# Chunk-select attention and a gated MLP on one core: an earlier load order, more k, q and v buffers, a new order of all engines, and a last output tile in two halves

## The chip, the core and the metric

The kernel runs on one core of one Trainium2 chip. Its engines work side by side: TensorE (PE: matmuls, and PEld: its weight loads), VectorE (DVE), ScalarE (ACT), GpSimd (POOL, which here issues all loads) and SyncE (SP, which here issues transposing transfers, copies between buffers and stores). The metric is the device time of one execution in microseconds, the median of several runs.

## The reference, cut to what is computed

Inputs: q, k, v of shape (4, 8, 768, 64), and weights w_in (512, 1024), w_spatial (768, 768), b_spatial (768), w_out (512, 512), all float32. Output: (4, 768, 512) float32.

```python
k_min, k_max = k_chunks.min(3), k_chunks.max(3)            # 24 chunks of 32 keys
ub = sum_d max(q * k_min, q * k_max)                        # a bound for each query and chunk
top_chunks = argsort(where(causal_chunk, ub, -1e9))[..., -6:]
scores = where(in_top_chunks & causal, q @ k.T / 8, -1e9)
x = softmax(scores) @ v                                     # heads side by side: (4, 768, 512)
h = relu(x @ w_in);  u, v = h[..., :512], h[..., 512:]
v_n = (v - mean(v)) / sqrt(var(v) + 1e-6)
v_s = einsum('ts,bsd->btd', w_spatial, v_n) + b_spatial[:, None]
out = (u * v_s) @ w_out
```

## The kernel before, in words

**Tiling.** Tokens go in tiles of 128, so a sequence has six. Heads are worked in pairs: 16 pairs i, four to a batch (0 to 3 are batch 0), two to a load group g = i // 2. After four pairs have filled a batch's x, the MLP of that batch runs while the pairs of the next batch go on. The MLP of the last batch has nothing beside it.

**The order is written out by hand.** The string ORDER is a list of short names, and each name stands for one small function that issues one or a few instructions on one engine. The kernel body ends with a loop that calls them in this order. Each engine then works through its own names strictly in that order, and waits where an operand or a buffer is not there yet. Engines are tied only by data and by buffers. The function build lists each name with its engine, its dependences and the buffers that it takes; PLAN holds its parameters (buffer counts, and a list of names, `flip`, whose engine is exchanged between ACT and DVE).

**The names**, for pair i, head hi (0 or 1) and batch b, with lines of the kernel before:

- Loads on POOL: `lk`, `lq`, `lv` with g and, for k and q, a half (L589, L595, L600; eight smaller ones for g = 0 at L604), `win` (eight, L608), `wsp` (six, L624), `wout` (four, L626), `lb` (L627). The k loads go into 4 buffers, q into a ring of 4, v into a ring of 4. A q buffer also holds the selection bits beside q, whose place `ring` (DVE, L532) clears once; `small` sets a column of ones in each v buffer (L546) and some constants.
- Bounds: `kT` transposes k on PE (L665; `kTb` again into another bank for pairs 0 and 1, L674), `kmax` and `kmin` reduce it to chunks (DVE, L686), `kb` spreads them (L708), `qT` transposes q (L722; `qTb` L679), `rq` takes its positive and negative parts (L731, L733, or ACT), `ub` multiplies (L742), `top` finds the eight largest of each row (DVE, L752), `sel` compares and writes the selection next to q (L778).
- Operands of the scores: `kop` copies k.T (L717) or, from pair 8 on, `kc` copies it (L703) and `kop` moves it on by a transfer from SP (L715); `kh` puts the mask rows into the k operands once (L574). `aT` transposes q with its selection on PE (L797; `aTA`, `aTB` in parts for pair 0, L785), `ac` copies it (L800; L790, L792 for pair 0); from pair 8 on one transposing transfer `aTd` on SP does both (L803).
- Attention: `sc` scores in six strips (L810, and L813 for the triangle in batch 0), `ex` exp (ACT, L819), `tri` clears the upper triangle from batch 1 on (POOL, L825), `av` in three parts (L836), `rc` and `nm` normalise (DVE, L841, L846), `x` brings x.T to the MLP (transfer on SP, L855; for pairs 0 to 3 and 15 `xp` on PE, L861, and a DVE copy, L864).
- MLP, tile ti: `v` and `u` (x times w_in), `s` (times w_spatial), `o` (times w_out), all matmuls at L930; `va` and `ua` relu on ACT (L947, L962); `bs`, `vs`, `rs`, `vn` normalise; `gt` the gate on DVE (L973, three buffers), `gd` its transposing transfer on SP (L988; for the last two tiles `gp` on PE and a copy, L980, L986), `oc` copies the output out of PSUM (L993), `os` stores it (L997). `wsT` and `wsc` transpose w_spatial once (L634, L636).
- `dm`: matmuls of zeros into a spare bank, 65 of them, between the first instructions of PE (L873).

**What sets the order around the change.** POOL issues loads and triangles in one order, so a load that stands behind a triangle waits for that pair's exps. SP issues `aTd`, `kop`, `x`, `gd` and `os` in one order. PE, DVE and ACT likewise. PSUM has 3 banks for scores, 1 for small transposes and bounds, 1 for av, 3 for the MLP and, in batch 0, for transposes.

Of the kernel before, what the change touches and what calls it, by code (L numbers as in the profile page):

```python
# [166 lines left out]
def mmc(n): return max(n/2.4+2.5,25)/1000  # L167
DEF=dict(BEATS=12,pa=8,dve_a=(),qx=('ACT',),xp=4,mlp_first=13,mlp_mul=1.0,sc=3,tr=1,acc=1,ml=3,kbuf=3,qbuf=3,vbuf=3,ebuf=3,late=240,chunk=2,
  lk=40,lq=36,lv=18,kdma=99,kcp=2,kcdma=1,kc_act=(),shift=4,prep=0.0,tm=.8,lm=0.2,lm2=1.2,gp=(),head=1,lag=0.0,kp=27,ca=99,tree=0,svk=1.4,svw=1.15,flip=(),wide=0,pt=(),xd=(),dum=0,warm0=0.,qa_dve=(),ma_act=(),mkbuf=2)
PEL=0.2  # L170
def build(prm=None):
# [19 lines left out]
    for x in range(2):  # L191
        for hi in range(2):
            op(f'lk0{hi}{x}','POOL',.815,acq=[('k',0)],prio=B0-1+2*x+.1*hi,dma=(.85,1.8))
            op(f'lq0{hi}{x}','POOL',.815,acq=[('qs',0)],prio=B0-.5+2*x+.1*hi,dma=(.85,1.8))
# [16 lines left out]
    for i in range(NPAIR):  # L211
# [34 lines left out]
        for hi in range(2):  # L246
            if (kd or kc) and p['kcdma']:
                op(f'kop{i}{hi}','SP',.5,deps=[kt],acq=[('kh',i)],uses=[kr],prio=pr((3 if hi==0 else 8)),dma=(.45,1.8))
            else:
                ke='ACT' if i<2 else 'DVE'  # L250
                kq=('acc',f'kb{i}') if kdup else kr
                op(f'kop{i}{hi}',ke,(.80 if ke=='ACT' else .46) if not tree else .30,.1,deps=[f'kTb{i}' if kdup else kt],acq=[('kh',i)],uses=[kq],prio=pr((3 if hi==0 else 8)))
# [69 lines left out]
    for b in range(B):  # L322
# [5 lines left out]
        o_=[group('o',b,ti,4,lambda c0,m,ti=ti: [f'gd{b}{ti}']+[f'wout{j}' for j in range(KO)],[('gT',f'{b}{ti}')]) for ti in range(NQT)]  # L328
# [32 lines left out]
    for b in range(B):  # L361
        for ti in range(NQT):
            q=s.ops[last('o',b,ti,4)].prio
            op(f'oc{b}{ti}','ACT',.465,.12,deps=[last('o',b,ti,4)],acq=[('o',f'{b}{ti}')],uses=[('ml',f'o{b}{ti}')],prio=q+.5)
            op(f'os{b}{ti}','SP',.5,deps=[f'oc{b}{ti}'],uses=[('o',f'{b}{ti}')],prio=q+.6,dma=(.7,1.6))
# [6 lines left out]
    for o in s.order:  # L372
        if o.name[:2]=='kh': o.alts=('DVE',.32)
        elif o.name[:3]=='kop' and o.eng=='ACT': o.alts=('DVE',.46)
        elif o.name=='rq01' and o.eng=='ACT': o.alts=('DVE',.40)
    for n in p['flip']:
        o=s.ops[n]; e,oc=o.alts; o.alts=(o.eng,o.occ); o.dur+=oc-o.occ; o.eng,o.occ=e,oc
    for k in range(p['dum']): op(f'dm{k}','PE',mmc(128),PEL,deps=['dz'],acq=[('sc','dm')] if k==0 else [],uses=[('sc','dm')],prio=-22+k*.15)
# [3 lines left out]
PLAN = {'late': 40, 'mlp_first': 8, 'qbuf': 4, 'kbuf': 4, 'vbuf': 4, 'dum': 65, 'warm0': 5.3, 'kcp': 8, 'flip': ['ac21', 'ac60', 'ac71', 'gd34', 'kc11', 'kc13', 'kc14', 'kc9', 'kh01', 'kh31', 'oc00', 'oc01', 'oc11', 'oc12', 'oc13', 'oc20', 'oc22', 'rq01'], 'gp': ((3, 4), (3, 5)), 'lm': 0.2, 'lm2': 1.2, 'tm': 0.8}  # L382

ORDER = """
dz id0 dm50 ring0 dm19 dm26 lk000 dm35 dm14 dm55 dm53 ring1 dm13 dm36 dm49 lk010 dm6 dm1 small dm46 dm60 ring2 lq010
ring3 lq000 id1 lk011 expand lk001 kT0 kh31 kh30 dm40 dm7 lq001 dm56 dm31 dm3 kmin0 dm62 kTb0 kh21 lq011 qT0 kmax0
kh20 dm27 dm10 dm15 qTb0 lk10 dm42 dm38 dm41 dm48 kh01 dm30 dm8 dm57 kop01 rq00 rq01 mlat kop00 kT1 lk11 kb0 dm54 dm11
dm43 dm44 dm24 kmax1 dm32 dm52 dm45 kh00 dm0 ub0 kTb1 lv0 top00 dm20 dm47 dm2 dm23 kh11 dm34 dm29 dm58 dm59 dm28 kmin1
dm4 dm5 dm25 dm63 dm61 dm39 dm64 dm22 qT1 kh10 mtri dm18 dm33 dm21 top01 dm51 dm37 dm17 dm16 selA0 kop10 lq10 sel0
aTA00 rq11 aTB0 dm12 rq10 dm9 kop11 lq11 acA00 aTA01 kb1 sc000 acB0 ub1 lk20 ex000 sc001 top10 sc002 ex001 sc004 acA01  # L390
kT2 lq20 ex002 top11 sc003 ex004 sel1 sc011 kop20 lk30 av000 ex003 sc005 kop21 ex011 sc013 kmax2 lq21 aT10 ex005 ex013
aT11 av001 kmin2 ac10 sc010 lk21 av002 ex010 sc100 rc00 kb2 qT2 nm00 ac11 win01 kT3 rq21 sc015 wsp3 sc012 ex100 rq20
qT3 wsp5 ex015 kmax3 sc102 ex012 sc014 lv1 ex102 sc112 kmin3 ub2 ex014 av010 sc101 ex112 top20 sc111 lk41 ex101 av011
rq31 sc103 av012 ex111 top21 sc104 lk31 rc01 ex103 sel2 sc113 kb3 ex104 rq30 sc105 aT20 nm01 ex113 sc115 lv2 ub3 kop31
ex105 av100 ac20 sc114 top30 av101 sc110 ex115 kop30 ex114 av102 lq30 sc203 top31 ex110 aT21 rc10 sel3 sc200 ex203
nm10 win30 sc202 qT4 ex200 ac21 kT4 ex202 win21 sc205 rq40 sc201 aT30 kmax4 ex205 ex201 sc215 sc212 av110 ex215 win00
kmin4 ex212 sc211 av111 sc210 ac30 av112 rq41 aT31 ex211 kb4 sc204 kop40 ub4 ex210 sc214 kop41 ex204 rc11 sc213 top40
kT5 ex214 lq31 nm11 sc300 ac31 xp0 top41 av200 kmin5 ex213 av201 sc301 ex300 av202 sel4 xp1 ex301 rc20 sc310 kmax5
sc311 wsp2 ex310 qT5 sc302 win31 nm20 ex311 sc303 rq51 ex302 av210 rq50 ex303 av211 kop51 sc305 aT40 ex305 kop50 av212
sc304 ac40 x0 sc313 kT6 win20 rc21 ex304 kb5 aT41 nm21 sc315 ex313 sc312 kmax6 ex315 sc404 ac41 win11 sc314 x1 xp2  # L400
ex312 win10 av300 kmin6 ub5 ex404 av301 sc401 lk61 ex314 top50 sc402 av302 ex401 sc403 top51 wsp0 rc30 ex403 sc400
sel5 nm30 ex402 aT50 kop61 av310 ac50 lk40 x2 av311 sc412 ex400 kop60 sc405 qT6 av312 kb6 ex412 wsp4 sc415 rq60 kT7
ex405 rc31 sc413 ex415 rq61 sc411 tri40 sc501 nm31 ex413 aT51 kop70 ex411 av400 lq41 xp3 kmax7 ac51 av401 sc410 av402
wsp1 ex501 x3 sc414 ub6 ex410 kmin7 sc502 v00.0 ex414 sc503 kop71 ex502 v00.2 tri41 rc40 sc504 top60 sc500 v02.0 ex504
nm40 wout1 v04.0 ex503 top61 lq40 av410 va00 sel6 v02.2 qT7 lk50 va02 v04.2 rq71 av411 ex500 sc514 rq70 av412 va04
sc511 bs00 aT60 ex514 v01.0 rc41 ac60 ex511 sc510 v03.0 vs00 kb7 ex510 bs02 sc600 ub7 ex600 v01.2 nm41 sc505 sc515
top70 v03.2 x4 ex505 va01 av500 top71 tri50 sc513 ex515 sc603 sel7 va03 wsT0 bs01 wout0 ex513 av501 aT61 wsc0 ex603
lv3 av502 sc602 wsT1 rc50 ac61 vs02 bs04 sc512 v05.0 ex602 wsc1 aT70 ex512 kT8 nm50 sc613 ac70 v05.2 kmin8 tri51 sc604
sc601 va05 av510 vs04 lk71 kc8 u01.0 ex604 kmax8 av511 ex601 qT8 lv4 u01.2 ex613 rq81 u00.0 ua01 vs01 rq80 sc611 sc605
sc610 bs03 ex611 lq50 u00.2 aT71 bs05 ua00 av512 wsT2 kb8 ex605 sc614 ac71 wsT3 tri60 ex614 wsc2 sc704 ub8 ex610 wsc3  # L410
wsT4 lk51 u02.0 vs05 ex704 rc51 vs03 top80 sc703 rs0 u02.2 lq51 nm51 ex703 sc612 wsT5 wsc4 ex612 av600 lb top81 sc701
ua02 sc700 vn04 u03.0 ex701 wsc5 sc702 av601 ex700 vn00 u04.0 ex702 vn01 u03.2 sel8 av602 sc615 u04.2 ua03 vn03 aTd8
kT9 ex615 vn02 ua04 sc705 s00.0 tri61 rc60 ex705 nm60 sc710 kc9 sc713 vn05 s00.2 tri70 kop80 ex710 av610 kmin9 x5
sc715 s00.4 ex713 wout2 u05.0 kmax9 lq60 av611 kop81 sc711 av612 qT9 kop90 ex711 rc61 s01.0 nm61 ex715 u05.2 rq91
av700 rq90 ua05 s01.2 kb9 sc714 gt00 av701 ub9 ex714 sc712 gd00 av702 top90 s02.0 rc70 s01.4 top91 sc803 sel9 kop91
s02.2 gt01 ex803 sc800 aTd9 kT10 ex712 nm70 s02.4 ex800 kmin10 sc805 qT10 tri71 ex805 sc801 gd01 sc810 kmax10 s03.0
ex801 wout3 av710 ex810 sc802 gt02 x6 sc804 av711 ex802 sc812 kc10 av712 ex804 s03.2 rc71 ex812 s04.0 kop100 nm71
tri80 sc814 kb10 gd02 sc815 rq101 kT11 ex815 s03.4 lq61 rq100 ex814 sc811 kmax11 av800 x7 ex811 s04.2 gt03 av801 sc813
av802 ub10 kop101 ex813 rc80 s05.0 kc11 sc900 tri81 sc905 sc901 nm80 s05.2 kop110 ex901 top100 lk60 s04.4 ex900 gd03
av810 gt04 s05.4 ex905 av811 sc911 kmin11 sc904 o00.0 ex911 av812 gt05 ex904 sc903 sc910 o00.2 top101 ex910 sc912  # L420
sel10 o02.0 ex903 oc00 aTd10 qT11 ex912 o01.0 rq111 sc902 rc81 o02.2 kb11 ex902 rq110 kop111 o01.2 nm81 oc02 ub11 gd04
tri90 v10.0 oc01 sc913 v11.0 lq70 x8 v10.2 v13.0 lv5 va10 sc914 v11.2 bs10 v13.2 va11 av900 v14.0 ex913 bs11 av901
va13 v12.0 top110 ex914 sc1002 av902 top111 v14.2 ex1002 bs13 o03.0 va14 v12.2 rc90 sel11 sc915 vs10 sc1000 nm90 va12
kT12 aTd11 o03.2 vs11 ex1000 kc12 v15.0 ex915 bs14 oc03 sc1003 tri91 sc1001 gd05 av910 kmin12 ex1001 v15.2 lq71 u10.0
# [35 lines left out]
def kernel(  # L460
# [407 lines left out]
    for n in range(prm["dum"]):  # L868
        @act(f"dm{n}")
        def warm(n=n):  # L870
            if "warm" not in tiles:
                tiles["warm"] = ps_sc.tile([P, 512], F32, tag="sc", name="warm")
# [135 lines left out]
    for b in range(B):  # L1008
        mlp(b)
# [33 lines left out]
```

## Time and profile before

| | |
|---|---|
| median of 6 runs | 204.19 us (202.82 to 204.53) |
| the profiled execution's own time | 205.19 us |
| its span, first to last instruction | 203.5 us |
| granted TensorE clock, mean | 0.995 |
| PE / DVE / ACT / POOL busy | 189.5 / 157.6 / 147.4 / 79.7 us |
| HBM read, written | 24.38 MB, 6.29 MB |

The profile is of one execution. Its page gives, for each engine, the busy time, then the span in 40 slices of about 5.1 us with the busy share of each in tenths, then the chain of work that ended last, followed back from the end, then the costliest groups of instructions. The trace behind it can be asked for a stretch of time, for the waits of an engine, and for the time from the issue of a transfer to its landing. A line such as `87.67 7.06 DMA gT<-g` of the chain means that from 87.67 us on the chain spent 7.06 us on that transfer. In a wait line the numbers are the total time, how often, and the longest.

### The profile page before, as it was taken

The page shows a single profiled execution, that of the slowest core. Times are in us where ns is not written, and L with a number is a line of the kernel's source. Part 1 is how long each engine was busy: PE and PEld are TensorE (multiplying, and loading weights), DVE is VectorE, ACT ScalarE, POOL GpSimd, SP SyncE. Part 2 cuts the span into 40 slices and gives each one's busy share as a digit, 9 for nine tenths or more (in the row PEclk, how much of TensorE's full clock was granted, in tenths as well). Part 3 has the DMA queues.
Part 4 walks back from the last instruction along what each step waited for, and adds up shares of the span by engine and source line. Part 5 has one row for each costly group of instructions (what it writes and reads, how often), then busy time and mean ns, then how long its engine had stood idle before and what let it go on. Part 6 is the DMA issues. An engine that isn't in the chain of part 4 may idle for free.

```text
span 203.5 us, 5218 instructions
## 1 busy us (share of the span) xinstructions
PE 189.5 (93%) x2012; PEld 119.2 (59%) x2012; DVE 157.6 (77%) x476; ACT 147.4 (72%) x292; POOL 79.7 (39%) x96
## 2 busy tenths in 40 slices
PE   3897999999999999997999999999899999999991
PEld 2885678767576756663555655565455555444440
DVE  6898899999899999986688968795687466467530
ACT  2877999899799994875498958688799470564142
POOL 7999774257637853360614321304303030000000
PEclk9999999999999999999999999999999999999998
DMA  6999999999999999999999997969964172250355
GB/s 41 104 128 152 156 165 140 165 176 151 123 110 104 142 119 185 153 171 136 144 147 154 155 251 197 100 170 175 174 156 152 26 193 59 73 208 0 72 187 209
DMA packets 114617, 28.60 MB, mean 141 GB/s; under 512 B 108704, under 2 KB 111008, under 8 KB 114592
## 3 DMA queue, kind: packets, MB, share of 16 engines
q0 software_dynamic: 76544, 12.20, 91.6%
q1 hardware_dynamic: 38048, 16.06, 37.8%
q8 instruction: 16, 0.26, 0.6%
q14 instruction: 9, 0.07, 0.1%
HBM read 24.38 MB, written 6.29 MB: 151 GB/s over the span
## 4 chain that ended last, share of the span: by engine, by line
PE 62%; DVE 17%; DMA 11%; POOL 4%; ACT 2%; issue 1%; SPq 1%; POOLq 0%; DVEq 0%
PE mlp L930 40%; PE sc L810 10%; PE acc L836 7%; DVE kmm L686 4%; DMA vt<-in_v_dram 4%; DMA gT<-g 3%; DMA a<-qs 3%; DVE kh L717 3%; DVE max L752 2%; DVE x L846 2%; POOL qs L604 2%; POOL k L604 2%; PE kTp L665 1%; PE trq L722 1%; PE ub L742 1%
## 5 line engine op out<-in xcount | busy, mean ns | idle before, releaser
L819 ACT ACTIVATE e<-sc 128x512 f16<-128x512 f32 (+1 forms) x192 | 94.5, 559 | 21.7 <-PE sc L810 18.2
L810 PE MATMUL sc<-a,kh 128*128 128x512 f16 (+3 forms) x256 | 61.4, 305 | 0.8 <-DMA a<-qs 0.5
L930 PE MATMUL mlp<-w_in_sb,xT 128*128 128x512 f16 x192 | 51.9, 379 | 0.0
L825 POOL TENSOR_SCALAR_AFFINE_SELECT e<-e 128x768 f16<-128x768 f16 x24 | 21.1, 884 | 75.6 <-ACT e L819 48.5
L836 PEld LDWEIGHTS <-e 128*128 128x128 f16 x672 | 31.4, 97 | 15.2 <-issue 2.2
L930 PE MATMUL mlp<-vn,wsT 128*128 128x512 f16 x144 | 38.8, 379 | 0.1
L836 PE MATMUL acc<-vt,e 128*128 128x65 f16 x672 | 35.8, 194 | 1.4 <-DMA vt<-in_v_dram 0.9
L686 DVE TENSOR_REDUCE kmm<-kTp 128x24 f16<-128x768 f16 x32 | 29.6, 950 | 2.1 <-ACT kT L703 1.0
L810 PEld LDWEIGHTS <-kh 128*128 128x128 f16 x256 | 22.8, 97 | 13.9 <-issue 1.0
L973 DVE SCALAR_TENSOR_TENSOR g<-mlp,b_col,u 128x512 f16<-128x512 f32 x24 | 17.9, 748 | 13.4 <-PE mlp L930 10.8
L930 PE MATMUL mlp<-w_out_sb,gT 128*128 128x512 f16 x96 | 26.4, 379 | 0.4 <-DMA gT<-g 0.4
L930 PEld LDWEIGHTS <-xT 128*128 128x128 f16 x192 | 16.9, 97 | 14.6
L952 DVE BATCH_NORM_STATS2 stats<-vraw 128x6 f32<-128x512 f32 x24 | 16.3, 682 | 7.0 <-ACT vraw L947 7.0
L993 ACT COPY o<-mlp 128x512 f32<-128x512 f32 x17 | 9.9, 589 | 14.2 <-PE mlp L930 14.2
L947 ACT ACTIVATE vraw<-mlp 128x512 f32<-128x512 f32 x24 | 14.5, 603 | 5.7 <-PE mlp L930 5.7
L930 PEld LDWEIGHTS <-wsT 128*128 128x128 f16 x144 | 12.5, 97 | 10.2 <-DVE vn L967 0.3
L846 DVE TENSOR_TENSOR x<-acc,rec 128x384 f16<-128x384 f32 x32 | 17.6, 550 | 0.5
L962 ACT ACTIVATE u<-mlp 128x512 f16<-128x512 f32 x24 | 14.1, 600 | 4.6 <-PE mlp L930 4.5
L752 DVE MAX8 max<-ub 128x8 f32<-128x8 f32 (+4 forms) x160 | 15.5, 166 | 1.8 <-PE ub L742 1.6
L595 POOL DMA_DIRECT2D qs<-in_q_dram x14 | 14.5, 1035 | 2.1 <-DMA vt<-in_v_dram 2.1
L589 POOL DMA_DIRECT2D k<-in_k_dram x14 | 14.5, 1039 | 1.9 <-DMA qs<-in_q_dram 1.8
L930 PEld LDWEIGHTS <-gT 128*128 128x128 f16 x96 | 8.8, 97 | 9.1 <-DMA gT<-g 0.9
(76 smaller groups left out, 232.9 us busy)
## 6 DMA issues: line engine op xcount, KB each, us to landing
out_dram<-o SPq DMA_DIRECT2D x24, 256.0 KB, 2.5
vt<-in_v_dram POOLq DMA_DIRECT2D x8, 384.0 KB, 8.7
k<-in_k_dram POOLq DMA_DIRECT2D x14, 192.0 KB, 6.8
qs<-in_q_dram POOLq DMA_DIRECT2D x14, 192.0 KB, 7.1
kh<-kT SPq DMA_DIRECT2D x16, 96.0 KB, 4.3
ws_raw<-in_moe_w_spatial_dram POOLq DMA_DIRECT2D x6, 192.0 KB, 7.9
w_in_sb<-in_moe_w_in_dram POOLq DMA_DIRECT2D x8, 128.0 KB, 8.8
w_out_sb<-in_moe_w_out_dram POOLq DMA_DIRECT2D x4, 128.0 KB, 3.4
```

Source lines behind the costliest of these rows:

```text
L589: nc.gpsimd.dma_start(out=k_tile(g)[:, :, :, hi, :].rearrange("p x t d -> p (x t) d"), in_=source(k, b, 2 * hp + 2 * hi, 2))
L595: nc.gpsimd.dma_start(out=t.rearrange("p x t d -> p (x t) d"), in_=source(q, b, 2 * hp + 2 * hi, 2))
L686: nc.vector.tensor_reduce(self.kmm[:, m, :], src.rearrange("d (c ch) -> d c ch", ch=CHUNK), axis=AX.X, op=op, negate=(m == 1))
L752: nc.vector.max(self.max8[:, qi - 1, hi, :], self.ub[:, c0:c0 + CPT * (qi + 1)])
L810: mm(sc[:, col:col + n], lhsT=self.kh[hi][:, t * P:(t + 1) * P], rhs=self.a[:, q0 // P:(q0 + n) // P, hi, :], start=True, stop=not diag)
L819: nc.scalar.activation(out=self.e[hi][:, g * 512:g * 512 + width], in_=self.sc[hi, g][:, 0:width], func=Act.Exp, scale=scale)
L825: nc.gpsimd.affine_select(out=blk, in_=blk, compare_op=Alu.is_ge, fill=0.0, base=0, channel_multiplier=-1, pattern=[[0, NQT], [1, P]])
L836: mm(self.av[hi][:, qi, :], lhsT=self.e[hi][:, c:c + P], rhs=self.v[hi][:, t, 0:D + 1], start=first and n == 0, stop=last and n == len(blo ...
L846: nc.vector.tensor_tensor(self.x16[:, :, hi, :], in0=self.av[hi][:, :, 0:D], in1=self.rec[hi].to_broadcast([P, NQT, D]), op=Alu.mult)
L930: mm(st[kind, ti], lhsT=lhsT, rhs=rhs, start=(j == 0), stop=(j == n - 1))
L952: nc.vector.bn_stats(st["stats", ti], st["vraw"][:, ti, :])
L973: nc.vector.scalar_tensor_tensor(g, in0=st["s", ti], scalar=b_col[:, ti:ti + 1], in1=st["u"][:, ti, :], op0=Alu.add, op1=Alu.mult)
```

## The change

The PLAN of the kernel after has `kbuf` 6 (was 4), `qbuf` 5 (was 4), `vbuf` 6 (was 4), another list of flips, and two new entries, `dum0` 42 and `split` 1. The costs with which build was run have other values in places; they reach the chip only through the order.

```diff
-PLAN = {'late': 40, 'mlp_first': 8, 'qbuf': 4, 'kbuf': 4, 'vbuf': 4, 'dum': 65, ... 'flip': ['ac21', 'ac60', 'ac71', 'gd34', 'kc11', 'kc13', 'kc14', 'kc9', 'kh01', 'kh31', 'oc00', 'oc01', 'oc11', 'oc12', 'oc13', 'oc20', 'oc22', 'rq01'], ...}
+PLAN = {'late': 40, 'mlp_first': 8, 'qbuf': 5, 'kbuf': 6, 'vbuf': 6, 'dum': 30, ... 'flip': ['ac10', 'ac41', 'ac51', 'ac60', 'ac71', 'gd34', 'kc10', 'kc12', 'kc13', 'kc9', 'kh00', 'kh11', 'kop00', 'kop40', 'kop71', 'oc01', 'oc03', 'oc13', 'oc21'], ... 'dum0': 42, 'split': 1}
```

- The zero matmuls: one block `dm` of 42 at the start, and 30 single ones later in the head.

```diff
+    acts["dm"] = lambda: warm(prm["dum0"])
     for n in range(prm["dum"]):
-        @act(f"dm{n}")
+        acts[f"dm{n}"] = lambda: warm(1)
```

- The last output tile (batch 3, tile 5) is made in two halves of 256 columns: `o35.0`, copied by ACT (`oc35`) and stored by `os35`; then `o35.2`, copied by DVE (`od35`) and stored by `ot35`.

```diff
+            def o_half(n):
+                st["oh", n] = ps_ml.tile([P, 512], F32, tag="mlp", name="mlp")
+                for db in range(KO):
+                    mm(st["oh", n][:, 0:half], lhsT=st["gT", ti][:, db, :], rhs=w_out_sb[:, db, n * half:(n + 1) * half],
+                       start=(db == 0), stop=(db == KO - 1))
...
+                copier("DVE" if n else "ACT")(st["osb", ti][:, n * half:(n + 1) * half], st["oh", n][:, 0:half])
...
+                nc.sync.dma_start(out=out[b, ti * P:(ti + 1) * P, n * half:(n + 1) * half],
+                                  in_=st["osb", ti][:, n * half:(n + 1) * half])
```

- ORDER is new throughout. POOL's part of it, first before and then after, from the second load group on (the first eight loads and the small constants come ahead of it in both):

```diff
-lk10 lk11 lv0 lq10 lq11 lk20 lq20 lk30 lq21 lk21 win01 wsp3 wsp5 lv1 lk41 lk31 lv2 lq30 win30 win21 win00 lq31 wsp2 win31 win20 win11 win10 lk61 wsp0 lk40 wsp4
-tri40 lq41 wsp1 tri41 wout1 lq40 lk50 tri50 wout0 lv3 tri51 lk71 lv4 lq50 tri60 lk51 lq51 lb tri61 tri70 wout2 lq60 tri71 wout3 tri80 lq61 tri81 lk60
-tri90 lq70 lv5 tri91 lq71 lv6 tri100 lk70 tri101 tri110 tri111 tri120 tri121 lv7 tri130 ...
+lk11 lk10 lv0 lq10 lq11 wsp0 win00 lk20 lk21 lq20 lq21 lv1 lk31 win21 win11 lk30 wsp4 win01 lv2 wsp5 lq30 lq31 win30 win20 win31 win10 wsp1 lk40 wsp2 lq40
+tri40 wsp3 tri41 lq41 lk41 lk51 lq61 tri50 lv3 lb lv4 lq50 lq51 lk61 tri51 lk50 tri60 tri61 lk60 wout1 tri70 tri71 wout3 wout2 tri80 wout0 lv7
+tri90 tri81 lq60 lv5 lq71 tri91 lk71 lk70 tri100 tri101 lv6 tri110 lq70 tri111 tri120 tri121 tri130 ...
```

DVE's order in the head, before and after:

```diff
-dz id0 ring0 ring1 small ring2 ring3 expand kh31 kmin0 kmax0 kh01 rq00 rq01 kb0 kmax1 top00 kmin1 top01 selA0 sel0 rq11 rq10 acA00 kb1 acB0 top10
+dz id0 ring3 ring2 ring0 expand kh00 ring4 ring1 kh11 kmin0 kmax0 small kb0 rq00 kop00 kmax1 top00 kmin1 selA0 top01 kb1 sel0 rq11 rq10 acA00 acB0 top10
```

PE's order in the head and into pair 0's scores (`dm` stands for any number of zero matmuls):

```diff
-dm kT0 dm kTb0 qT0 dm qTb0 dm kT1 dm ub0 kTb1 dm qT1 dm aTA00 aTB0 dm aTA01 sc000 ub1 sc001 sc002 sc004 kT2 sc003 sc011 av000 sc005 sc013 aT10 aT11 av001
+dm kT0 dm kTb0 dm qTb0 dm qT0 dm kT1 ub0 kTb1 dm qT1 aTA00 aTB0 dm ub1 sc000 sc001 aTA01 sc002 sc005 kT2 sc004 sc013 sc011 aT10 sc003 sc010 av000 aT11 sc015 av001
```

SP's order in the stretch of the first MLP:

```diff
-x4 aTd8 kop80 x5 kop81 kop90 gd00 kop91 aTd9 gd01 x6 kop100 gd02 x7 kop101 kop110 gd03 aTd10 kop111 gd04 x8 aTd11 gd05
+x4 x5 aTd8 kop80 kop81 kop91 x6 gd00 kop90 aTd9 gd01 gd02 x7 gd03 kop101 aTd10 kop100 gd04 gd05 kop110 aTd11 kop121 x8
```

The end of the lists:

```diff
-... o34.2 oc33 o35.0 oc34 os33 o35.2 os34 oc35 os35
+... oc33 o35.0 o34.2 os33 oc35 o35.2 oc34 os35 od35 os34 ot35
```

Two optional paths that PLAN does not use (`pt`, `kdm`) are added as well; they issue nothing.

## Prediction

> **What bounds the kernel now.** First the page's busy rows and slices: they say which engine has no room in which stage.
>
> ```profile
> PE 189.5 (93%) x2012; PEld 119.2 (59%) x2012; DVE 157.6 (77%) x476; ACT 147.4 (72%) x292; POOL 79.7 (39%) x96
> ...
> PE   3897999999999999997999999999899999999991
> ...
> DVE  6898899999899999986688968795687466467530
> ```
>
> PE is busy in all but the first slices and slices 18 and 19 (about 92 to 102 us). "Busy" counts pipelined ends, so I worked with starts: a 512-column matmul starts every 0.216 us, a 128-column one every 0.056, an av one (L836) every 0.030, a score one (L810, L813) by its columns at the same rate. All useful matmuls at these pitches make 177.3 us; the last starts at 199.0. (The pitches are the usual distances between two starts in the trace; a sum of them is what I call PE work.) So some 22 us are lost in front of or between them, and those alone can be won. Start time minus work done so far grows like this: 11.7 us at the first score (14.86), 14.4 at 22 us, 15.3 at 34, 18.8 at 54, 19.0 just before 89, 21.1 at 96.4, 21.9 from 145 to the end.
>
> Second, the stage windows and the chain of waits for what causes the growth. The columns of the windows are length, PE, PEld, DVE, ACT and POOL busy.
>
> ```profile
> 25.00:50.00 25.00, 23.86 (x379) 18.51 (x378) 24.52 (x86) 24.14 (x51) 14.06 (x19) 1.00 2.25 162
> 50.00:90.00 40.00, 39.77 (x493) 26.45 (x490) 38.49 (x119) 33.56 (x69) 22.29 (x26) 1.00 1.47 136
> 87.00:97.00 10.00, 8.39 (x92) 4.81 (x90) 7.19 (x22) 6.30 (x13) 2.71 (x3) 1.00 1.51 157
> ```
>
> From 25 to 50 us DVE has 0.5 us free: there DVE sets the pace. From 50 to 90 PE does, with DVE 1.5 us behind.
>
> ```profile
> 11.12 7.78 DMA vt<-in_v_dram
> ...
> 87.67 7.06 DMA gT<-g
> 94.83 0.75 DVE g L973
> ...
> 138.46 6.69 DMA a<-qs
> ...
> 199.43 0.58 ACT o L993
> ```
>
> These are four places: a v load that the first av waits for; gd02 (a transpose of the gate), which lands 0.05 us before o02.0 should start and also keeps DVE's next gate waiting, as its buffer is not free; aTd14; the tail. The wait rows between 85 and 100 us price the second:
>
> ```profile
> DVE g L973 <- DMA gT<-g: 1.9, 1, 1.9
> ...
> PE trq L722 <- DVE qs L778: 1.0, 1, 1.0
> ```
>
> gT transposes take 2.4 us from 156 to 176 us, with no load in flight, and up to 7.7 beside loads. So waits follow from which load is out when.
>
> **The change, part by part.** For every SP transfer and load I summed, in both orders, the PE work at the pitches above between the place where it is issued and its first reader: its lead. Lead minus transit is slack. In before, the only transfers after 30 us with under 0.5 us of slack by this reckoning are gd02 (lead 7.39, transit 7.06) and aTd14 (5.94, 6.69), the two that the chain shows; so leads are a usable measure.
>
> *Loads.* The loads in front of POOL's first triangle (tri40) are about the same set in both orders, some 41 us of landings. What is left behind pair 6's triangles (75 us in before) is also nearly equal: wout2, wout3, lq60, lq61, lk60, lq70, lq71, lk70, lv5, lv6, lv7 before; wout0, wout2, wout3, lq60, lq70, lq71, lk70, lk71, lv5, lv6, lv7 after. So buffers do not shorten the stream; they exchange members. What counts: lv7 leaves 138.5 us, where it took 9.15 us and aTd14 beside it 6.69. Two more v buffers and one q buffer cost 2 x 0.07 us (L546) and 0.70 us (L532 row) of DVE in the head.
>
> *Head.* DVE's work ahead of sc000 grows from 12.3 to 13.6 us (ring4 0.70, two kh copies and kop00 come over, two kh copies and rq01 leave, acB0 is drawn in front). By hand, with durations from the rows: expand ends at 5.25, kh00, ring4, ring1, kh11 fill DVE to 7.5, the two reductions to 9.3, small, kb0, rq00, kop00 to 11.2, kmax1, top00, kmin1 to 13.4, selA0 to acA00 to 15.6. So the first exp starts near 16.1, against 15.33. That is covered: the next gates are landings, and they stand in the same place (lk1x 16.9, lv0 18.9, lq11 21.4); av000 is now behind sc003 and sc010, so lv0 blocks no scores, and ac10 (0.7) leaves ACT. rq21 starts at 22.0 in both. I take 0; bounds -0.3 and +0.8 (nothing recovered).
>
> *The opening 42 matmuls.* They run 107 ns apart from 1.06 to about 5.6 us, where PE only waited for lk (5.81 at the earliest), and add nothing. In before, the spacing falls from 107 to 56 ns at 10.4 us, 4.6 us after steady work began at 5.81; afterwards a stretch with about a third of PE's time used (16.1 to 19.5) did not slow it. In the changed head PE is unused at most 2.1 us (11.6 to 13.7, waiting for selA0). I price it 0.
>
> [...]
>
> *25 to 54 us.* Between nm10 and x3 the lists hold 20.6 us of DVE work before and 19.5 after (ac21 and kop40 go to ACT, kop70 is put off, ac41 comes). ACT gets 0.6 us more, with 0.9 free. PE's work ahead of v00.0 is 33.05 and 32.81. DVE-bound, v00.0 can come 1.1 us sooner. I take -0.8, as DVE's in-order waits also move; bounds -1.6 (the whole difference and its 0.5 of idle) and +0.8.
>
> *75 to 100 us.* gd02's lead becomes 10.98: slack 3.9 at the old transit, so the losses at 89.4 (0.27), 94.8 (0.67) and 96.4 (1.21), 2.15 in sum, lose their cause. What is late next: wout0 now goes out 5.5 ahead of o01.0 (the first of the o matmuls; wout rows took 2.9 to 4.4); gd01 has 7.2 (4.5 to 7.7), x7 6.9 (3.8 to 6.7), kop100 5.8 (2.9 to 6.2), lq60 6.9 ahead of qT12 (4.1 to 7.4), each with lv7, the wouts or lv5 beside it. Each has slack at its middle row, none at its worst. I take half of the win lost again: -1.1; bounds -2.15 and +1.0 (two of the worst rows in sequence).
>
> *145 us.* aTd14's lead grows to 6.9 and no load runs beside it (rows without loads: aTd15 3.7), so 0.68 goes. kop140 now has 3.6 (2.2 without loads). I take -0.5; bounds -0.7 and +0.5.
>
> *Tail.* Matmul columns are the same. In before the last copy is 0.58, then the store (issue 200.04, landing 2.09 later). After, half a copy on DVE ends about 0.35 after the last matmul, but ot35 is queued on SP behind os34, whose issue ends about 0.5 after it; 0.15 is won there, and half the bytes may land sooner. I take -0.2; bounds -0.35 and +0.1 (two stores that hinder each other).
>
> Other moved copies (kc, oc, ac51) lie where DVE and ACT have room by the slices; 0.
>
> Sum: 0 - 0.8 - 1.1 - 0.5 - 0.2 = -2.6. The profiled execution took 205.19 with a span of 203.5, and the median of the six runs is 204.19; taken from the span it gives 200.9, from the median **201.6**.
>
> **Rivals.**
> 1. *The gain is eaten by new waits.* The late stream is no shorter, and leads of 5.5 to 7 replace one of 7.4. If one or two of those five bite for as much as the old ones did (2.15) and DVE's win in 25 to 54 halves to 0.4, only 0.4 + 0.5 + 0.2 stay: 203.1; with aTd14's win lost to kop140 also, 203.6. For it: the equal list of loads. Against it: slack at every middle row.
> 2. *Slower: lq60.* It stands on POOL behind tri90 and tri81, which end when pair 8's and 9's exps do, and in front of it are lv7 and the wouts. qT12 waits for it, and all PE work behind in order. Price: transit minus 6.9. With the 201.6 of the rest, before's time is reached at a transit of 9.5 us and +0.5% at 10.5; loads took up to 12.25 us in this trace (lv2, at 28 us, eight in flight), which would make 206.9. Against it: q loads after 60 us took 5.3 to 7.4.
> 3. *The change does less than it says*: DVE's order has new in-order waits from 25 to 54 (+0.8 in place of -0.8), and everything else holds: 203.2.
>
> **How the numbers follow.** About 0.5% (1.0 us) is what a measurement of this kernel can tell from no change. Forecast 0.52 (own range 200.2 to 202.9); rival 1 0.18 and rival 3 0.12 (together 203.1 to 204.6, a third of it still over 0.5% faster); rival 2 0.10 (205 to 207); more than the forecast (all low bounds near, under 200) 0.08. Faster: 0.52 + 0.08 + 0.10 = 0.70; same 0.20; slower 0.10. For 8 in 10 the range leaves out most of rival 2 and the far low end: 199.8 to 204.9.
>
> **What would show it.** Right: the chain has no gT or a transposition of 7 us at 87 and 138; PE's start minus work is about 18.0 at v00.0, grows by at most 1.2 up to 100 us, and by under 0.2 at 145; the first exp is near 16. Wrong: a PE wait for wout, x7's xT, kop100 or lq60's qs between 85 and 112 us; DVE under 24 us busy between 25 and 50; matmuls 107 ns apart after 12 us.

## The result and the profile after

The kernel after takes 203.95 us (median of 38 runs, 202.67 to 206.59); the kernel before took 203.98 on the same chips (78 runs, 202.48 to 206.32). The ratio is 1.0007, with a 95% interval of 0.9992 to 1.0022. (Ratios leave out executions more than 1.5% above the fastest of their kernel; medians and ranges keep them.) That is no change, where I had forecast 201.6 us, 1.3% faster.

The two profiled executions differ by more: 205.19 before and 203.56 after. Most of that is the luck of the draw. Before's profile lies 1.2 us above its median, after's 0.4 us under its own. So a step is only trusted below where several traces agree.

The page of the kernel after, to be laid beside the lines of before in the prediction:

```profile
PE 190.9 (95%) x2023; PEld 121.1 (60%) x2023; DVE 157.7 (78%) x477; ACT 147.8 (73%) x295; POOL 79.5 (39%) x96
...
PE   7759999999999999999999999999999999999992
...
PEclk9978999999999999999999999999999999999998
```

and before's row of the clock:

```profile
PEclk9999999999999999999999999999999999999998
```

PE is busier, the hole in slices 18 and 19 is gone, and the last row has something that before's has not: a granted clock of 0.7 to 0.8 of full speed in slices 2 and 3 (10 to 20 us). (Ahead of the first opening that a trace records, 10.46 us in before and 6.12 in after, the row stands at 9, although the matmuls are 107 ns apart there.) The stage windows of after (length, then PE, PEld, DVE, ACT, POOL busy, granted clock, DMA share, GB/s):

```profile
10.00:15.00 5.00, 2.68 (x32) 2.11 (x33) 4.94 (x21) 3.47 (x5) 4.92 (x7) 0.79 1.90 124
15.00:20.00 5.00, 4.94 (x64) 3.99 (x61) 4.23 (x18) 3.18 (x8) 5.00 (x7) 0.86 2.29 162
...
25.00:50.00 25.00, 23.76 (x375) 18.39 (x372) 24.58 (x87) 24.41 (x51) 11.86 (x17) 1.00 1.75 157
50.00:90.00 40.00, 40.00 (x492) 26.36 (x489) 38.84 (x119) 33.23 (x69) 23.18 (x25) 1.00 1.71 139
87.00:97.00 10.00, 9.02 (x94) 5.21 (x91) 7.96 (x25) 7.12 (x15) 4.13 (x5) 1.00 1.65 136
```

and the first two of them in before:

```profile
10.00:15.00 5.00, 4.56 (x77) 4.12 (x75) 4.33 (x19) 3.98 (x5) 4.92 (x7) 1.00 1.95 126
15.00:20.00 5.00, 3.51 (x53) 2.62 (x52) 4.41 (x17) 3.69 (x8) 5.00 (x6) 1.00 2.41 152
```

From 10 to 15 us PE was busy 4.56 us before, mostly with zero matmuls, and 2.68 after. The granted clock is then half from 12.94 to 16.36. From 87 to 97 PE still misses 1.0 us. The chain of waits of after says for what (start, length, what):

```profile
87.99 8.34 DMA xT<-x
...
105.86 8.65 DMA xT<-x
...
195.88 2.14 DMA out_dram<-o
```

gd02 (gT) and aTd14 have left the chain, as forecast, and so has the first v load. In their place stand x7 and x8, two transposes of attention's output on SP. Before's wait for a gT is replaced by these rows, one for x7 and one for x8. In the second it is DVE that waits, and PE behind it:

```profile
PE mlp L950 <- DMA xT<-x: 1.0, 1, 1.0
DVE x L862 <- DMA xT<-x: 1.3, 1, 1.3
```

The prediction's measure, start time minus PE work done, in the profile of every kernel (names of the experiments below; sc115 starts near 27 us, v00.0 near 51, v10.0 at 93 to 98, s10.0 some 20 us on, o30.0 near the end):

| profile | sc115 | v00.0 | v10.0 | s10.0 | s20.0 | o30.0 |
|---|---|---|---|---|---|---|
| before | 14.97 | 18.50 | 21.09 | 21.13 | 21.89 | 21.91 |
| b_again | 14.27 | 17.89 | 21.12 | 21.16 | 21.88 | 21.91 |
| b_thin | 15.19 | 18.70 | 19.46 | 19.50 | 20.83 | 20.86 |
| b_g4 | 14.56 | 18.10 | 19.43 | 19.47 | 19.91 | 19.94 |
| b_loads | 14.44 | 17.95 | 18.95 | 18.99 | 21.78 | 21.81 |
| after | 14.34 | 18.03 | 18.45 | 20.15 | 20.46 | 20.51 |
| a_again | 14.97 | 18.65 | 19.00 | 20.38 | 20.91 | 20.97 |
| a_warm | 14.37 | 18.05 | 18.94 | 21.26 | 21.97 | 22.03 |
| a_spread | 15.64 | 19.32 | 19.67 | 19.73 | 20.27 | 20.33 |
| a_both | 13.53 | 17.20 | 17.56 | 17.62 | 18.16 | 18.22 |
| a_both2 | 13.78 | 17.47 | 17.84 | 17.90 | 18.44 | 18.50 |
| a_buf4 | 13.72 | 17.41 | 17.78 | 17.84 | 18.39 | 18.44 |
| a_nosplit | 13.65 | 17.34 | 17.68 | 17.74 | 18.29 | 18.34 |
| a_warm_lv7 | 13.54 | 17.21 | 17.55 | 18.24 | 20.33 | 20.38 |

After loses 1.7 us between v10.0 and s10.0, where the two xT are late (1.14 us at 96.4, 0.5 at 115.2).

### The profile page after: what moved, and what is told of

Read it like the earlier page. It is cut to its first block, busy times and chain, and to the rows that moved or that the text cites. A ratio compares the mean times of both kernels' runs of the same rounds, so it can differ in the third digit from the quotient of the medians.

```text
span 201.9 us, 5240 instructions
## 1 busy us (share of the span) xinstructions
PE 190.9 (95%) x2023; PEld 121.1 (60%) x2023; DVE 157.7 (78%) x477; ACT 147.8 (73%) x295; POOL 79.5 (39%) x96
## 4 chain that ended last, share of the span: by engine, by line
PE 66%; DVE 17%; DMA 9%; ACT 2%; issue 2%; POOL 1%; SPq 0%; POOLq 0%; ACTq 0%
PE mlp L950 39%; PE sc L826 12%; DMA xT<-x 8%; PE acc L852 8%; DVE kmm L697 4%; DVE max L768 2%; DVE kh L733 2%; PE tra L813 1%; PE ub L758 1%; PE kTp L673 1%; PE trq L738 1%; DVE x L862 1%; DMA out_dram<-o 1%; DVE rq L747 1%; PE wtr L642 1%
## 5 line engine op out<-in xcount | busy, mean ns | idle before, releaser
L835 ACT ACTIVATE e<-sc 128x512 f16<-128x512 f32 (+1 forms) x192 | 93.5, 562 | 18.9 <-PE sc L826 15.1
L1013 ACT COPY o<-mlp 128x512 f32<-128x512 f32 x19 | 11.1, 589 | 16.9 <-PE mlp L950 16.6
L857 DVE RECIPROCAL rec<-acc 128x6 f32<-128x6 f32 x32 | 6.0, 187 | 10.1 <-PE acc L852 10.0
```

The costliest lines, as they stand in the source:

```text
L835: nc.scalar.activation(out=self.e[hi][:, g * 512:g * 512 + width], in_=self.sc[hi, g][:, 0:width], func=Act.Exp, scale=scale)
```

## Experiments

**Theory.** The change brings about what was forecast, and two losses eat it: the clock that falls to half in the thinner head (some 0.8 us), and xT transposes that travel beside a crowd of late loads (some 1.6 us). **Rivals**: that there was little to win, because before's late gd02 is a chance of the one execution that was profiled; that the added buffers matter and not the order. Experiments whose name begins with b change the kernel before, those with a the kernel after. Ratios are to the kernel before on the same chip, intervals are 95%.

**1. Both kernels once more** (no edit).

> The kernel before, unchanged, for a second profiled execution. Theory 1 (chance of the baseline): the profiled execution that the prediction was made from took 205.19 us, 1.2 above the kernel's median of 203.98, and part of its 2.15 us of lost PE time between 89 and 96.4 us is not there in a usual execution; then this one has a span near 202.3 and loses at most 1 us there. Theory 2 (the gain is eaten by new waits of the kernel after): the losses at gd02 and aTd14 are usual, so this one again loses 1.5 us or more at 89 to 97 and 0.5 at 145, and its span is 203 or more when its own time is. Against itself the time is a ratio of 1.000 by both.

> The kernel after, unchanged, for a second profiled execution. Theory 2 says that its own losses are usual: the clock closes for one 3.4 us stretch in the head again, or nearly so (the mean clock differs between executions), the v matmuls of batch 1 wait about 1 us for x7 near 96 us. Theory 1 expects no certain place. Ratio to before 1.000, interval about 0.997 to 1.003.

b_again 1.0016 [0.9985, 1.0047], a_again 1.0012 [0.9979, 1.0046]. b_again's profile has gd02 out from 87.52 for 7.25 us and DVE waiting 1.8 us for it, as before's has. a_again's has the clock at half from 14.57 to 17.98 and xT of x7 and x8 out for 8.05 and 8.50 us. So both the old loss and the two new ones come again in a second trace. (b_again's, too, is of an execution 1.2 us slower than the median of its kernel, so it does not tell whether a usual one loses as much.) Over executions the clock is plainer still: the mean granted clock was at least 0.993 in all runs of before on the chips of the experiments and 0.979 to 0.992 in all 38 of after. By this measure not one execution of after kept its clock.

**2. The clock alone: 26 more zero matmuls** in the kernel after, where PE had little to do.

```diff
-'dum': 30
+'dum': 56
 PE: ... kT1
+dm30 ... dm37
 ub0 kTb1
+dm38 ... dm55
 qT1 ...
```

> The kernel after with 26 more zero matmuls on PE in the head: 8 behind kT1 and 18 behind kTb1, where PE was mostly unused from 9.9 to 13.1 us before the clock fell to half at 12.94. They do no work that the output needs. Theory 2: the clock stays open, the ten fillers, ub1 and the first scores run at 56 ns and sc000 starts near 15.6 instead of 16.35; if the head's loss is carried to the end, 0.5 to 0.9 us less than the kernel after (ratio to before about 0.996). Rival: the landings of lv0 and lq11 and DVE set the pace at 20 us anyway, the 0.7 us are absorbed, and the time stays at 1.000 within 0.2%.

0.9908 [0.9877, 0.9938], 202.81 us. Work that computes nothing made the kernel 0.9% faster, more than the 0.996 that was expected. Its windows:

```profile
10.00:15.00 5.00, 3.77 (x65) 3.18 (x63) 4.94 (x21) 3.56 (x5) 4.93 (x7) 1.00 1.87 120
15.00:20.00 5.00, 4.94 (x79) 4.01 (x77) 4.91 (x20) 3.99 (x9) 5.00 (x7) 1.00 2.30 160
```

The clock stays at 1.00, in all 12 executions at 0.996 or more, and the first score starts at 15.54 in place of 16.35. The profile is of its slowest execution (205.07), so past the head it says little; in it the gain at the first score is already lost again at sc115 (14.37), because a transpose of q waits 1.0 us for its load. In it x7 and x8 are still out for 8.0 and 10.2 us: this edit mends one loss, not the other.

**3. The same in reverse: before without its 33 zero matmuls between kT1 and aTA00.**

> The kernel before without the 33 zero matmuls between kT1 and aTA00 (they do no work that the output needs); 32 stay. If thin work on PE in the head is what closes the clock, the clock falls to half once between 12 and 17 us here too, the mean clock goes from 0.995 and more to 0.98 to 0.992, and the time rises by 0.5 to 1.3 us (ratio 1.003 to 1.006). Rival (the clock is closed by something else in the kernel after, such as its opening block of 42 or its order): no closing, ratio 1.000.

0.9958 [0.9921, 0.9995], 203.89 us. The clock did fall, from 15.05 to 18.46 in the profile and, by the mean clock of 0.989 to 0.992, in 8 of the 12 executions; yet the time did not rise, it even went down a little. In the profile sc115's delay is 15.19, against 14.97 and 14.27 in before and b_again, so the head lost 0.2 to 0.9 us. But gd02 landed at 93.07, 5.1 us after its issue, and the loss at 94 to 96 us did not occur: from v00.0 to v10.0 the delay grows by 0.76 in place of 2.59 and 3.23. Then aTd14 costs 1.1 us in place of 0.5. Why gd02 landed sooner stays open. Nor do its executions with a fallen and with a kept clock differ clearly (medians 203.9 and 203.6 us). So this run is a miss: it shows that the clock falls with a thin head in the old order too (0.66 granted from 15 to 20 us), and does not show what that costs.

**4. The crowd alone: wout and lq60, lv5, lv7 moved on POOL's list** of the kernel after, so that the loads behind tri80 to tri91 no longer leave in one bunch.

```diff
-tri40 wsp3 tri41 ... wout1 tri70 tri71 wout3 wout2 tri80 wout0 lv7 tri90 tri81 lq60 lv5 lq71 tri91
+tri40 wsp3 lv5 lq60 tri41 ... wout1 wout3 wout2 wout0 tri70 tri71 tri80 tri90 tri81 lv7 lq71 tri91
```

> The kernel after with only POOL's loads placed otherwise: lv5 and lq60 go out behind wsp3, where POOL had nothing to load (48.9 to 52.5 us); wout0, wout2 and wout3 directly behind wout1 (76 us); lv7 behind tri81 (95 us) instead of 86.4. Theory 2: x7 has no load beside it at 88 us and lands in 5 us or less instead of 8.34, the wait of 1.14 us at 96 goes, as does x8's part at 115 (0.53); 1.0 to 1.6 us less than the kernel after (ratio to before about 0.993 to 0.995). Rival (DVE and ACT are nearly full from 20 to 95 us, so PE only gets its wait elsewhere): under 0.4 us less.

0.9920 [0.9893, 0.9946], 203.38 us. No wait of PE is left between 85 and 118 us; xT of x7 and x8 take 4.2 and 5.5 us. From v10.0 to s10.0 the delay grows by 0.06 in place of 1.7. The head is as in after, or worse: six of its 11 executions stand at a clock of 0.98 (two half-speed stretches of 3.41 us, from 12.85 to 19.68 in the profile) and take 203.4 us; four at 0.992 take 202.5 to 203.3; the one at 0.999 takes 201.92. So a stretch at half speed costs 0.6 to 0.8 us here, and this kernel prices it without any edit of the head. After's own 38 executions agree: the 13 with a mean clock of 0.979 to 0.983 have a median of 204.7 us, the 25 with 0.987 to 0.992 one of 203.8.

**5. Both edits**, and the same kernel once more on another chip.

> The kernel after with both edits at once: the 26 more zero matmuls in the head and the loads spread (lv5 and lq60 behind wsp3, wout0, wout2, wout3 behind wout1, lv7 behind tri81). If the clock that closes in the head and the transfers that land late beside loads are two causes that add, the ratio to before is near 0.985 (0.991 and 0.992 were measured for one each), the mean clock is 0.996 or more in every execution, and the executions spread by little. Rival: the two share a cause (a head that is late makes the transfers collide elsewhere); then about 0.991 again.

> The kernel after with both edits once more, beside the three others on one chip, as their base and for more executions of the fastest version. Ratio 0.984 to 0.990, mean clock 0.995 or more in all, no PE wait of over 0.35 us behind 50 us in the profile.

0.9871 [0.9835, 0.9907] and 0.9868 [0.9834, 0.9902]: 201.49 and 201.46 us, the size that was forecast for the change itself. In the profile PE has no gap left in the stretch of the first MLP:

```profile
87.00:97.00 10.00, 10.00 (x104) 5.84 (x101) 8.45 (x33) 7.42 (x16) 4.12 (x4) 1.00 0.77 112
97.00:117.00 20.00, 19.95 (x210) 12.07 (x209) 17.87 (x53) 17.72 (x36) 6.18 (x6) 1.00 1.44 184
```

The time comes out as the two edits say: against after, a_both's delay is 0.81 less at sc115 (the clock) and 2.53 less at s10.0, so 1.7 less again from the transfers; 0.24 of it is given back by s20.0. In medians the two edits bring 0.9% and 0.8% of 204 us singly and 1.3% together. That is 0.4% less than the sum, but the intervals of the three ratios are as wide as that, so whether the two overlap is not settled. The executions also lie closer together (201.37 to 202.28, six of them, against 203.14 to 206.35 for 29 of before on that chip). That an order with slack at each transfer loses less by chance would explain it; it was not tested.

**6. lv7 late again**: a_warm, with lv7 back behind tri121 as in before.

> The kernel after with the 26 zero matmuls and with lv7 alone moved, back to where the kernel before has it (behind tri121). It tells which load matters. If it is lv7 beside x7 and gd02, x7 lands in 6 us or less and the wait near 96 us goes, 0.5 to 1.0 us less than the zero matmuls alone (ratio near 0.987), with a new wait for aTd14 of up to 0.7 near 140 us, as in the kernel before. If it is the crowd of lq60, lv5, lq71, lk71 and lk70 between 95 and 103 us (x8 8.65, aTd11 10.25 us), the waits at 112 to 116 us stay and the ratio is 0.990 or more.

1.0004 [0.9964, 1.0044], 204.39 us against 202.81 of a_warm. Its chain:

```profile
139.23 4.95 DMA kh<-kT
```

lv7 is out from 136.70 to 143.39, a kop transfer (kT to kh) beside it takes 4.95 us, and PE loses 1.8 us at 144.2; neither case expected a loss of that size. x7 lands in 4.9 us (8.0 in a_warm) and its wait is gone, so lv7 is what delayed x7. x8 still takes 8.8 us, and from v10.0 to s10.0 the delay grows by 0.7. By the two ratios the early lv7, one part of the change, is worth 1% of the time in this order. Not all of that need be the transfer: in four of the 12 executions the mean clock was 0.988 to 0.992 in spite of the 26 zero matmuls, and these took 206.4 to 207.6 us, the other eight 203.5 to 204.9. Where the clock fell in the four, no trace shows.

**7. Only loads moved, in before**: lq60, lq61, lk60 ahead of tri50; wout2, wout3 behind wout0; lv7 behind lk70.

> The kernel before with only its loads moved, and its 4, 4 and 4 buffers kept: lq60, lq61 and lk60 ahead of tri50, wout2 and wout3 behind wout0, lv7 behind lk70. No load is then in flight from about 80 to 95 us and after 130 us. If late transfers beside loads cost before 2 us at gd02 and 0.7 us at aTd14 in a usual execution, the ratio is 0.988 to 0.993. If this needs the added buffers or DVE is the bound anyway, above 0.996.

1.0074 [1.0042, 1.0107], 206.24 us: slower. gd02 lands after 2.5 us and the old loss is gone, but a new one stands in the chain:

```profile
113.27 10.24 DMA a<-qs
```

aTd12 travels beside lv7 (112.36 to 123.68), and PE loses 2.7 us. Five of the 12 executions had a mean clock of 0.992 and took 206.1 to 208.1 us, the other seven 204.1 to 206.6; where it fell in the five, no trace shows. These early loads alone are no gain: the collision moved to another transpose.

**8. A fourth buffer for the gate, in before** (`tag="g"`, `bufs=3` to `bufs=4`): DVE's next gate no longer waits for gd02 to have left.

> The kernel before with a fourth buffer for the gate (one number: bufs 3 to 4 of the tile g), so DVE's gate of tile 5 no longer waits for gd02's landing. It asks whether the loss at 94 to 96.4 us, on which the prediction built 1.1 us, is there in a usual execution. In two of two profiles of the kernel before gd02 landed at 94.7 and DVE waited; in a profile of the thinned head it landed at 93.1. If the late landing is usual: ratio 0.993 to 0.996 (1.2 of the 1.9 us of DVE's wait come back to PE, the 0.6 of o02 stay). If it is rare, and the two profiles were chance: 0.998 to 1.001.

0.9944 [0.9915, 0.9972], 203.08 us. In its chain the gate stands behind DVE's own work, where before had gT in front of it:

```profile
87.95 0.86 DVE kmm L686
88.82 0.67 DVE g L973
```

If the late gd02 had been a chance of one profile, this would have done nothing to the median. It takes 1.0 us off, so a loss there is usual, though b_thin shows an execution without it. The 2.15 us that the prediction read off one execution may be more than a usual one loses.

**9. The buffers**: a_both with four q, four k and four v buffers, and without ring4.

> The kernel after with both edits (zero matmuls, spread loads), and with 4 k, 4 q and 4 v buffers instead of 6, 5 and 6; ring4 is gone from DVE's head. It asks what the added buffers are worth. Each load's place in POOL's order is the same, and by that order the buffer that it takes has been read before. If the order is what counts: the same as a_both (ratio 0.984 to 0.990), or up to 0.4 us less, as DVE's head is 0.83 us shorter. If buffers count (a load waits, and POOL's triangles behind it): 0.993 or more.

0.9892 [0.9859, 0.9925], 202.04 us. That is 0.2% from a_both, inside both intervals, and in the profile the clock stays open and no transfer is late. The added buffers themselves bring nothing that can be told.

**10. The last tile in one piece**: a_both with `split` 0 and the end of the lists as in before.

> The kernel after with both edits and the last output tile whole again, in the order o34.2, o35.0, o35.2 with one copy on ACT and one store. The prediction gave the halves 0.2 us, bounds -0.35 and +0.1. From the end of the last matmul's columns to the end of the span the profiles give 4.3 and 4.6 us before and 4.0 to 4.1 us after; so this one should have 4.2 to 4.7 and lose 0.2 to 0.5 us against a_both (ratio 0.001 to 0.002 higher, within the noise; the profile's tail decides).

0.9865 [0.9836, 0.9895], 201.49 us, the same as a_both. From the end of the last matmul's columns to the end of the span it is 4.13 us whole and 4.04 in halves (before 4.26, after 4.02).

## Why the prediction was wrong

**The step that failed first: "The opening 42 matmuls ... I price it 0".** It had two parts, and both were wrong. That PE would be "unused at most 2.1 us" holds for one gap, but the gaps add up:

```profile
10.63 0.42 PE L758 MATMUL ub<-km,rq 128*128 128x48 f16 x10 [0.67 <-DVE rq L747]
11.21 0.51 PE L682 MATMUL kTb<-identity,k 128*128 128x128 f16 x6 [0.16 <-DVE kh L733]
11.55 0.22 PE L888 MATMUL warm<-idle_op 128*128 128x128 f16 x1
13.15 0.69 PE L738 MATMUL trq<-identity,qs 128*128 128x128 f16 x5 [1.38 <-DMA qs<-in_q_dram]
...
14.82 1.27 PE L888 MATMUL warm<-idle_op 128*128 128x128 f16 x10
```

This is PE's timeline in after (start, length, what, and in brackets the idle time with its releaser). From 9.9 to 13.15 there is about 1 us of work; qT1 waits for its load, where I had PE waiting for selA0. The ten zero matmuls at 14.82 stand 107 ns apart again in place of 56, which was one of the signs named for "wrong". The second part was the argument that a stretch of before, 16.1 to 19.5, used to a third, had not slowed the clock. It was divided in the wrong places. In each of the four traces with a fall of the clock in the head, the changes come a multiple of 3.41 us after the opening: opened 6.12, half from 12.94 to 16.36 in after; 4.33 and 14.57 to 17.98 in a_again; 6.02 and 12.85 to 19.68 in a_spread; 11.63 and 15.05 to 18.46 in b_thin. I reckoned PE's use by these windows from the starts of its matmuls (where two starts lie more than 1.15 times the usual distance apart, what goes beyond the usual distance counts as unused). The windows at full clock that were used least while matmuls still ran before and after them, those of before's thin stretch, and one near the end:

| profile | window from | use | clock of the next window |
|---|---|---|---|
| after | 9.53 | 27% | half |
| a_again | 11.16 | 30% | half |
| b_thin | 11.63 | 33% | half |
| a_both (near the end) | 194.27 | 39% | full |
| a_spread | 9.44 | 39% | half |
| b_loads | 121.75 | 44% | full |
| a_warm_lv7 | 141.07 | 47% | full |
| a_again | 7.75 | 49% | full |
| before | 13.87 | 61% | full |
| before | 17.29 | 69% | full |

So of these windows at full clock those of 27 to 33% use were followed by half speed, those of 44% and more by full speed, and at 39% there is one of each. Whether use alone decides it was not shown. I had priced the thinner filler 0 on one stretch of one trace.

**Head, 0.** The instructions came as worked out by hand (kmin1 ends at 13.47, forecast 13.4; acA00 at 15.49, 15.6), and the sum is near 0, but from two terms. With the clock open, sc115's delay is 13.5 to 13.8 in five profiles of after's order (a_both, a_both2, a_buf4, a_nosplit, a_warm_lv7) and 14.4 in the sixth, a_warm, with its late q load. In before, b_again, b_g4 and b_loads it is 14.3 to 15.0. So the new head wins some 0.9 us, and in after the clock takes 0.8 of it. The clock also opens earlier, at 6.12 us in after, 4.33 in a_again and 6.02 in a_spread, against 10.46 in before and 11.63 in b_thin. Whether the opening block brings part of the 0.9 that way was not tried.

**25 to 54 us, -0.8.** Nothing was won there. From sc115 to v00.0 the delay grows by 3.5 to 3.6 us in all profiles of before's order and by 3.7 in all of after's; DVE is as full as it was, with 24.58 of 25 us. v00.0 at "about 18.0" came true (18.03) by luck: a win in the head that I had priced 0, and a loss to the clock, stand in for it.

**75 to 100 us, -1.1 (-2.15, +1.0): the second step that failed.** gd02's loss is gone, and b_g4 shows that there was one. But "each has slack at its middle row, none at its worst" understated the worst: x7's transit was to be 3.8 to 6.7 us against a lead of 6.9, and it was 8.34 beside lv7, wout0 and gd02. x8, on no list of mine, took 8.65 beside lq71, lk71 and lk70. Together they cost some 1.6 us. Transits were taken from rows with fewer loads in flight than the new order puts there. This is rival 1, down to one of its five names. lq60 (rival 2) was no trouble (5.94 us).

**145 us, -0.5.** From s10.0 to s20.0 the delay grows by 0.72 to 0.76 in before and b_again, 0.31 and 0.53 in after and a_again: 0.2 to 0.45 won. The mechanism holds: experiment 6 puts the load back and loses there (at a kop transfer, where before lost at aTd14).

**Tail, -0.2.** 0.24 between the two profiles, but 0.09 between a_nosplit and a_both, which differ in this alone. The direction is right; the size is not shown, and it is too small to be seen in a median.

**The sum.** It was -2.6 us, and the median did not move. The clock, priced 0, and the two late xT are the terms that ate it: 0.8 and 1.6 us in the profile, and a kernel without them runs at the forecast time. That it does so exactly is partly luck. The -0.8 of 25 to 54 us was not there, the 0.9 of the head stands in its place, and the 2.15 us at gd02 came from an execution 1.2 us slower than the median. (The 200.9 "from the span" is itself a span; the time of that execution was 1.7 us longer.) Giving rival 1 a chance of 0.18 was too little, and the clock had no case at all.

## What to carry to other kernels

Price filler by what it holds up: before thinning it, divide the stretch into windows as long as the steps in which the clock changed (3.41 us in these traces), at every possible phase, as the openings here came anywhere from 4.33 to 11.63 us, and add up PE's use in each, gaps together. Where a transfer's slack is no larger than the spread of its transits, take its transit from a row with as many loads beside it as the new order will put there, and look at every transpose behind the moved loads, not only at the ones that were late. And look at a second execution of the kernel before, ahead of making sums from one: two profiles of one kernel pair differed by 1.6 us here where the medians did not differ.

## What the runs showed of the hardware

- The clock fell to half with PE in partial use: after windows of 3.41 us with 27, 30 and 33% use (after, a_again, b_thin) and with 39% (a_spread), not after another with 39% (a_both), and in these traces after none of 44% and more. The fall lasted 3.41 us (after, a_again, b_thin) or twice that (a_spread, 12.85 to 19.68).
- A transpose that takes 3.9 to 4.2 us in a_both and a_spread (x7), with no load in flight (0.77 and 0.92 in the DMA column of the window from 87 to 97 us), takes 8.0 to 8.3 in after, a_again and a_warm, beside lv7 and two transposes of the gate (1.65 in after). Loads took up to 13.0 us (lk70 in after), where the median of k loads in after is 7.0.
- The same transpose at the same place of SP's order lands in 5.1 us in one profile, 6.2 in another and 7.06 or 7.25 in two more (gd02 in b_thin, b_g4, before and b_again).
